# Weight-gradient chunks placed inside the last attention backward, and fourteen zero stores moved to the output phase

## The chip, the cores and the metric

The kernel runs on one core of one Trainium2 chip. A NeuronCore has five engines with an instruction stream each: TensorE (PE, with its weight loads shown apart as PEld), VectorE (DVE), ScalarE (ACT), GpSimd (POOL) and SyncE (SP), and 16 DMA engines that move data between the off-chip memory and the on-chip SBUF. Matrix products land in PSUM and are copied out of it by DVE or ACT. The metric is the device time of the whole program in microseconds (us); lower is better. Before the change it is 446.53 us, the median of 5 runs from 444.61 to 447.87 us.

## The reference

Two pre-norm layers, each an attention with a cached window and a dense block with a mish activation, are applied to a single token, twice, with the same weights; then everything is differentiated:

```python
def _fwd_reference(A_x, A_k_cache, A_v_cache, A_wq, A_wo, B_x, B_w1, B_b1, B_w2):
    def _A_ref(x, k_cache, v_cache, wq, wo):            # Hq 32, Hkv 4, Dh 128, Sk 32768
        W = min(4096, max(256, Sk // 4))                # only the last 4096 rows of the caches
        q = (lambda x, *d: x.transpose(*d))((x @ wq).reshape(B, Sq, Hq, Dh), 0, 2, 1, 3)
        k = jnp.repeat(k_cache[:, :, Sk - W:, :], rep, axis=1)
        v = jnp.repeat(v_cache[:, :, Sk - W:, :], rep, axis=1)
        scores = jnp.einsum("bhqd,bhkd->bhqk", q, k) * (Dh ** -0.5)
        p = _softmax(scores, axis=-1)
        o = jnp.einsum("bhqk,bhkd->bhqd", p, v)
        return (lambda x, *d: x.transpose(*d))(o, 0, 2, 1, 3).reshape(B, Sq, Hq * Dh) @ wo
    def _B_ref(x, w1, b1, w2):                          # D 1024, F 3584
        h = jnp.einsum("bsd,df->bsf", x, w1) + b1
        sp = jnp.log1p(jnp.exp(-jnp.abs(h))) + jnp.where(h > 0, h, jnp.zeros_like(h))
        return jnp.einsum("bsf,fd->bsd", h * jnp.tanh(sp), w2)
    x = A_x
    x = x + _A_ref(_layernorm(x), A_k_cache, A_v_cache, A_wq, A_wo)
    x = x + _B_ref(_layernorm(x), B_w1, B_b1, B_w2)
    ...
```

`reference` returns the output and the gradients of `A_x`, both caches, `wq`, `wo`, `w1`, `b1` and `w2`. With one token every weight gradient is a sum of two outer products (one for each use of the weight). The gradients of the caches are zero except in the last 4096 of 32768 rows, so the program must store 2 x 4 x 28672 rows of 128 bf16 zeros, 58.7 MB of the 170.13 MB that it moves.

## The kernel before, in words

The stages follow one another as a chain of small vectors: the forward layers A1, B2, A3, then `mlp_turn` (B4 forward and backward in one pass over `w1`), the backward of A3 (`attn_bwd` with `first=True`), a pass over `w2` (`W2Pass.rest`: the last forward product and the gradient of the hidden layer of B2), a pass over `w1` (`mlp_bwd_w1`), and the backward of A1 (`attn_bwd` with `first=False`), which ends in `g0`, the gradient of the input. In each stage the weights stream through a ring of 6 buffers of 512 KB (`st_tile`), loaded by SP's DMA queue. The kernel is written with the order of every engine's instructions by hand: what stands earlier in the code stands earlier in each engine's stream, and an engine takes its instructions in order.

**The zero stores.** The 112 zero stores of 512 KB each (128 rows of 4 KB) fill the DMA engines where a stage leaves them free. `bg_zeros(n, after)` (L180) issues n of them from POOL, after a tiny copy (`gate_t`) that waits for the tile `after`; `zeros(n)` (L167) issues them from SP; `zeros2(n)` (L171) takes two at once, 1 MB from a larger zero tile `area["zero"]`. The table `Z` (L1221) says how many go where: `B2a` and `B2` in the B2 stage, `A3`, `B4` by block of the B4 stage, `A3c` and `A3d` in the backward of A3, `B4w` by chunk of the `w2` pass, `W1m` by chunk of the `w1` pass, `A1c` and `A1d` in the backward of A1.

**The backward of A1** (L862 and on). It forms `do` from the incoming gradient `g_bf` and `wo` (functions `T` and `M`: transposes of the five `wo` chunks that are not kept, and products with them), multiplies it with V (`rows_mm`), forms `ds` from that (L990), multiplies `ds` with K (the PE line with `acc<-K`), copies the row, forms `dq` (L1011), multiplies it with `wq` (64 matmuls, `acc<-wq_b`), and ends in the layer norm's backward (`ln_bwd`). Beside that chain it prepares what the outer products need: `after_do` (L1195) cuts the SBUF space of `wo` into areas and clears two of them on POOL (L1200: the 2048 columns of the two spread tiles; L1202: the 4096 columns of `area["zero"]`); then five steps in the list `prep`, each of which is `spread_rows`: POOL copies a vector into a mostly zero spread tile, PE transposes it in 4 to 8 blocks (tile `rw`, L1046), and ACT copies the result to its place. `nextprep()` runs one such step after every `M` but the first, the last one after `rows_mm`. In gaps, `warm(n)` issues n matmuls of the identity with itself, whose result nobody reads.

**The output phase** begins after `g0`. PSUM is handed over to one pool of four pairs of banks (`pair`), and the list `jobs` runs: each job makes 4 matmuls (outer products with 2 rows of contraction), which fill two pairs, and two copies out of PSUM, one on DVE and one on ACT (`ev_out`), to half of a 1 MB staging slot, which SP stores after every second job; the jobs of `dkv` copy to their part of the tile `K`, which is stored in larger pieces. The jobs are, in this order: 14 for the gradient of `w2` (`dw_tall`, L1123) with 8 of the 16 for `w1` (`dw_wide`), the other 8 of `w1` woven with 8 of V's cache (`dkv`), 16 for `wo`, 16 for `wq` woven with 8 of K's cache. The gradient of K is stored only after its last job, 4 MB. Slots are taken in a ring: two in the space of `wo`, two of the weights' ring, two in V's space, and then the eight tiles of `wq_b`, put in after the last attention (L1315). The gradient of `wq` is staged in `wq_b` itself (`home`). The preparations for `wo`, V, K and `wq` (`late_prep`) stand between jobs.

Of the kernel before, what the change touches and what calls it, by code (L numbers as in the profile page):

```python
# [14 lines left out]
P = 128  # L15
HQ = 32
# [7 lines left out]
def kernel(  # L24
# [245 lines left out]

    def acc_tile(n):
        return pacc.tile([P, n], FP32, name="acc", tag="acc")

    def sm_tile(m, n):
        return pacc.tile([m, n], FP32, name="sm", tag="sm")

# [76 lines left out]
    def ln_bwd(dn_ps, n32, rstd, g_col, name, nxt):  # L353

        tt = work.tile([P, 2 * TD], FP32, name="tt")
        nc.vector.tensor_copy(tt[:, 0:TD], dn_ps)
        nc.vector.tensor_mul(tt[:, TD:], tt[:, 0:TD], n32[:])
        sps = sm_tile(P, 2 * TD)
        nc.tensor.matmul(sps[:], lhsT=onesD, rhs=tt[:], start=True, stop=True)
        if nxt == "A1":  # L360
            warm(5)
        if nxt == "B2":
            hook("ln")
        ab = work.tile([P, 2], FP32, name="ab")
        nc.vector.reduce_sum(ab[:], sps[:].rearrange("p (a b) -> p a b", a=2), axis=AX.X)
        t2 = work.tile([P, TD], FP32, name="t2")
        nc.vector.scalar_tensor_tensor(out=t2[:], in0=n32[:], scalar=ab[:, 1:2], in1=tt[:, 0:TD],
                                       op0=ALU.mult, op1=ALU.subtract, reverse1=True)
        gx = work.tile([P, TD], FP32, name="gx")
        nc.vector.tensor_scalar(out=gx[:], in0=t2[:], scalar1=ab[:, 0:1], scalar2=rstd[:, 0:1], op0=ALU.subtract, op1=ALU.mult)  # L370
        g_new = keep.tile([P, TD], FP32, name=f"g_{name}")
        nc.vector.tensor_add(g_new[:], g_col[:], gx[:])
        g_bf = pair_col("g" + nxt[0], nxt, TD)
        nc.vector.tensor_copy(g_bf, g_new[:])
        return g_new, g_bf
# [486 lines left out]
    def attn_bwd(g_col, g_bf, lname, sv, first, nxt):  # L862
# [30 lines left out]
        def M(i):  # L893
# [7 lines left out]
            if first and i in (1, 3, 5):  # L901
                fill(1, ["V", "K", "wq"], "a")
            if not first and i:
                nextprep()

# [10 lines left out]
        if not first:  # L916
# [6 lines left out]
                lambda: rows_put(area["R1"], 1, "dh", "pieces"),  # L923
            ])

        for i in range(2, len(late) + 1):
# [3 lines left out]
        if first:  # L930
            pre.extend(w2_load(c) for c in range(NB - 1))
            bg_zeros(Z["A3d"], g_bf)
            fill(100, ["V"])
        else:
            after_stream()
            zeros(Z["A1d"][0])
            zeros2(Z["A1d"][1])

# [30 lines left out]
        else:  # L969
            after_v()  # L970
            nc.sync.dma_start(area["p3"], out_5[0:P, :])
            nextprep(100)
            warm(3)
        scr = kp()
# [11 lines left out]
        dsT = kp().rearrange("p (j x) -> p j x", x=P)  # L986
        qrow = acc_tile(512)
        for hf in range(2):
# [3 lines left out]
        if first:  # L992
            fill(100, ["K"], "av")
        else:
            warm(4)
        for hf in range(2):
            half_T(ds, dsT, hf, "va"[hf])
        for j in range(TJ):
            for c in range(NC):
# [5 lines left out]
        else:  # L1005
            warm(3)
        qacc = sm_tile(P, HQ)
# [4 lines left out]
        if first:  # L1012
            fill(100, ["wq"], "av")
        nrow = acc_tile(512)
        for h in range(HQ):
            for half in range(2):
                row_mm(nrow, 2 * half + h % 2, dq_bf[:, h:h + 1],
                       wq_b[:, 4 * half:4 * half + 4, h // 16, (h % 16) * P:(h % 16 + 1) * P], h < 2, h >= HQ - 2)
        nps = sm_tile(P, TD)
        yr = rows_copy(nrow, "v")  # L1020
        if first:
# [14 lines left out]


    def spread_rows(n, put, dst, pairwise=False):

        sp = area["spread"][pools["sturn"] % 2]  # L1040
        pools["sturn"] += 1
        for l in range(2):
            put(sp.rearrange("p j (q x) -> p j q x", q=4), l)
        ps = psum1([P, 8, P], BF16, "rw")
        for j in range(n):
            nc.tensor.transpose(ps[:, j, :], sp[:, j, :], ident_bf[:])  # L1046
        o, i = dst, ps[:, 0:n, :].rearrange("p j x -> p (j x)")
        if pairwise:
            o, i = dst.rearrange("p (c x t) -> p c t x", x=P, t=2), ps[:, 0:n, :].rearrange("p (c t) x -> p c t x", t=2)
        evac(o, i, 0.69, 1.0, None if "pair" in pools else "a")  # L1050

# [143 lines left out]
    def after_do():  # L1195
# [3 lines left out]
        pools["sturn"] = 0  # L1199
        nc.gpsimd.memset(wo_flat[:, 0:2048], 0.0)  # L1200
        area["zero"], *more = cut_up(wo_flat, 8192, (4096,) * ((NR - 4) // 2))
        nc.gpsimd.memset(area["zero"], 0.0)  # L1202
        slots.extend(more)
# [12 lines left out]
    prep = []  # L1216
    def nextprep(n=1):
        for _ in range(min(n, len(prep))):
            prep.pop(0)()

    Z = dict(B2a=1, B2={0: 1, 4: 1, NW2 - 2: 4}, A3=14, B4=[3, 3, 2, 2, 2, 2, 5], A3c=6, A3d=28, B4w={1: 1, 4: 1, 13: 3}, W1=0, W1m=(8, 13), A1c=3, A1d=(7, 16))  # L1221

# [80 lines left out]

    g0, g0b = attn_bwd(g1, g1b, "A1", sA1, False, "X0")
    level()
    col_out(g0b, TD, out_1[0, 0, :])
    top(None)
    pacc.release()
    pt.release()
    pools["pair"] = ctx.enter_context(tc.tile_pool(name="pair", bufs=4, space=bass.MemoryType.PSUM))  # L1310

    def r3(nm):
        return area[nm].rearrange("p (g d) -> p g d", g=G)

    slots.extend(wq_b[:, t, :, :].rearrange("p h j -> p (h j)") for t in range(TD))  # L1315
    stage = {}

    def take(nm):
        stage[nm] = jobs[:]
        del jobs[:]  # L1320

    take("w")
    dkv(area["p3"], r3("do3"), sA1["p"], r3("do1"), out_3, True)
    take("v")
    dw_tall("wo", HQ, out_5.rearrange("(c p t) d -> c p t d", p=P, t=4))
    take("o")
    dkv(sA3["ds"], r3("q3"), sA1["ds"], r3("q1"), out_2, False)
    take("k")
    dw_wide(lambda: area["Rq"], 512, 2048, out_4, wq_t)
    take("q")  # L1330
    late_prep = [
        lambda: row_layout(sA3["dorep"], "do3"),
        lambda: row_layout(sA1["dorep"], "do1"),
        lambda: tall_left("wo", "o", 0),
        lambda: tall_left("wo", "o", 1),
        lambda: tall_right("wo", "gA"),
        lambda: row_layout(sA3["qrep"], "q3"),
        lambda: row_layout(sA1["qrep"], "q1"),
        lambda: rows_put(area["Rq"], 0, "nA", "rep"),
        lambda: rows_put(area["Rq"], 1, "dq", "heads"),  # L1340
        db1_out,
        x4_out,
    ]

    def weave(a, b, n):
        while a or b:
            jobs.extend(a[0:n])
            jobs.extend(b[0:1])
            del a[0:n], b[0:1]

    jobs.extend(stage["w"][:NW2 + 8])
    weave(stage["w"][NW2 + 8:], stage["v"], 1)
    jobs.extend(stage["o"])
    weave(stage["q"], stage["k"], 2)
    for at, f in zip((8, 11, 24, 27, 30, 40, 43, 46, 49, 51, 53), late_prep):
        jobs.insert(at, f)
    for at, n in ((24, 2), (27, 2), (33, 1)):
        jobs.insert(at, lambda n=n: zeros2(n))
    run(1000)
# [32 lines left out]
```

## Time and profile before

| What | Value |
|---|---|
| median of 5 runs | 446.53 us (444.61 to 447.87) |
| the profiled execution | 448.57 us |
| its span (first to last record) | 446.8 us |
| PE / DVE / ACT / POOL busy | 73% / 53% / 48% / 15% of the span |
| moved by DMA | 170.13 MB, mean 381 GB/s |
| zero stores from POOL / from SP in the backward of A1 / in the output phase | 84 / 24 / 4, in units of 512 KB |
| last copy out of PSUM ends | 432.34 us |
| last DMA ends | about 445.0 us |

The span is cut into stages by eye from the timeline: B2 from 68 to 112 us, A3 to 136, B4 to 196, the backward of A3 to 240, the `w2` pass to 264, the `w1` pass to 293, the backward of A1 to 333, and the output phase after it. In the rows of the profile, `out<-in` names the tile written and the tiles read; a bracket at the end of a timeline row says how long the engine was idle before it and what it waited for. PEclk is the clock that TensorE was granted, as a share of full speed. A DMA share near 1 means that all 16 DMA engines had packets in flight all the time.

### The profile page before, as it was taken

Reading aid. Unit: us, or ns where it says so; the run is one execution under the profiler, and the core shown is the slowest. Engines: PE = TensorE matmul, PEld = TensorE weight load, DVE = VectorE, ACT = ScalarE, POOL = GpSimd, SP = SyncE. Lnnn points to the kernel's source line nnn. Section 1 sums busy time; section 2 is a strip of 40 time slices with the busy share of each in tenths; the row PEclk is TensorE's granted clock in tenths of the full one; section 3 lists DMA queues with packets and bytes.
Section 4 is the critical chain, followed back from the end, with each engine's and each line's share of the span. In section 5 each row is a group of like instructions: output and inputs, shape, how many; then the busy total and the mean of one; then the engine's idle time right before and its main releaser. Section 6 shows DMA issues by size and latency. Waiting matters only on the chain. (4 is left out here: it accounts for less than half of the span.)

```text
span 446.8 us, 11638 instructions
## 1 busy us (share of the span) xinstructions
PE 324.2 (73%) x5020; PEld 222.3 (50%) x5020; DVE 235.2 (53%) x487; ACT 214.3 (48%) x253; POOL 66.4 (15%) x164
## 2 busy tenths in 40 slices
PE   1565755499898979898996577985967688675850
PEld 0343424389375979876875576864431132211110
DVE  3134101087252747675547473551439989897860
ACT  1122100065242857776855342523318877796860
POOL 2000000010520412242332010116010010000000
PEclk9989555565697988999998568867995555555555
DMA  7999999999999999999999999999978999999778
GB/s 319 422 420 414 407 399 375 385 347 387 373 406 355 370 352 351 376 409 407 415 407 382 416 350 366 298 400 419 425 316 343 419 418 413 396 415 395 307 305 352
DMA packets 44337, 170.13 MB, mean 381 GB/s; under 512 B 4449, under 2 KB 11645, under 8 KB 37501
## 3 DMA queue, kind: packets, MB, share of 16 engines
q1 hardware_dynamic: 31888, 124.79, 71.1%
q0 software_dynamic: 12352, 44.58, 25.5%
q8 instruction: 39, 0.64, 0.5%
q14 instruction: 14, 0.11, 0.1%
q10 hardware_dynamic: 44, 0.01, 0.0%
HBM read 70.27 MB, written 99.10 MB: 379 GB/s over the span
## 5 line engine op out<-in xcount | busy, mean ns | idle before, releaser
L278 PEld LDWEIGHTS <-ring 128*128 128x128 bf16 (+2 forms) x1828 | 60.0, 102 | 34.1 <-DMA ring<-in_B_w_dram 12.2
L195 ACT COPY ring<-tps 128x1024 bf16<-128x1024 bf16 (+1 forms) x40 | 37.6, 962 | 31.4 <-PE tps L242 31.2
L185 POOL DMA_DIRECT2D out_dram<-zt x84 | 44.5, 532 | 40.2 <-DMA out_dram<-zt 34.8
L242 PE MATMUL tps<-ident_bf,ring 128*128 128x128 bf16 x528 | 42.3, 240 | 4.9 <-DMA ring<-in_B_w_dram 4.8
L685 ACT COPY ring<-tps 128x1024 bf16<-128x1024 bf16 x28 | 28.3, 1012 | 31.6 <-PE tps L675 24.3
L698 DVE CUSTOM_DVE_ANT_0 ring<-ring,gbc 128x1024 bf16<-128x1024 bf16 x28 | 33.6, 1220 | 16.1 <-PE acc L278 15.1
L192 DVE CAST wq_b<-ops 128x1024 bf16<-128x1024 f32 (+1 forms) x36 | 39.2, 1126 | 4.4 <-DMA out_dram<-wq_b 2.7
L195 ACT CAST wq_b<-ops 128x1024 bf16<-128x1024 f32 (+1 forms) x40 | 38.3, 1014 | 5.6 <-PE ops L278 2.7
L242 PEld LDWEIGHTS <-ring 128*128 128x128 bf16 x528 | 35.6, 109 | 6.8 <-DMA ring<-in_B_w_dram 5.2
L278 PE MATMUL ops<-V 2*128 2x512 bf16 (+1 forms) x160 | 32.2, 603 | 5.7 <-DVE K L192 1.5
L192 DVE COPY ring<-tps 128x1024 bf16<-128x1024 bf16 (+1 forms) x30 | 19.6, 664 | 30.4 <-PE tps L242 30.3
L278 PEld LDWEIGHTS <-V 128*128 128x128 bf16 (+2 forms) x448 | 17.0, 102 | 33.0 <-issue 31.2
L278 PE MATMUL ops<-wo_b 2*128 2x512 bf16 x120 | 24.3, 557 | 8.2 <-ACT wq_b L195 3.0
L195 ACT COPY K<-tps 128x1024 bf16<-128x1024 bf16 x17 | 16.6, 1024 | 27.4 <-PE tps L242 27.4
L675 PE MATMUL tps<-ident_bf,ring 128*128 128x128 bf16 x224 | 25.6, 286 | 0.7 <-DMA ring<-in_B_w_dram 0.7
L278 PE MATMUL acc<-a_pair,ring 128*128 128x16 bf16 x448 | 15.9, 173 | 10.8 <-DMA ring<-in_B_w_dram 9.4
L192 DVE COPY K<-tps 128x1024 bf16<-128x1024 bf16 x15 | 10.2, 688 | 24.1 <-PE tps L242 24.1
L278 PEld LDWEIGHTS <-wo_b 2*128 2x128 bf16 (+1 forms) x232 | 9.1, 100 | 25.8 <-issue 23.6
L278 PE MATMUL q<-wq_b,nA_pair 128*32 128x512 bf16 x128 | 10.9, 465 | 14.9 <-DMA wq_b<-in_A_wq_dram 14.9
L195 ACT CAST K<-ops 128x1024 bf16<-128x1024 f32 x17 | 17.1, 1013 | 7.7 <-PE ops L278 7.5
L294 DVE COPY ring<-acc 128x512 f32<-128x512 f32 x6 | 4.1, 691 | 30.4 <-PE acc L278 30.4
L192 DVE CAST K<-ops 128x1024 bf16<-128x1024 f32 x15 | 18.3, 1221 | 3.3 <-PE ops L278 3.2
(319 smaller groups left out, 565.4 us busy)
## 6 DMA issues: line engine op xcount, KB each, us to landing
out_dram<-zt POOLq DMA_DIRECT2D x84, 512.0 KB, 10.1
ring<-in_B_w_dram SPq DMA_DIRECT2D x42, 512.0 KB, 7.7
ring<-in_B_w_dram SPq DMA_DIRECT2D x32, 448.0 KB, 6.4
out_dram<-wo_b SPq DMA_DIRECT2D x13, 1024.0 KB, 8.8
out_dram<-wq_b SPq DMA_DIRECT2D x12, 1024.0 KB, 5.1
ring<-in_A_wo_dram SPq DMA_DIRECT2D x20, 512.0 KB, 7.6
wq_b<-in_A_wq_dram SPq DMA_DIRECT2D x8, 1024.0 KB, 20.9
out_dram<-wq_b SPq DMA_DIRECT2D x7, 896.0 KB, 5.0
```

The lines of the kernel that those rows point to most:

```text
L185: nc.gpsimd.dma_start(zero_job(1), zt[:])
L192: nc.vector.tensor_copy(out_ap, in_ap)
L195: nc.scalar.copy(out_ap, in_ap)
L242: nc.tensor.transpose(ps[:, b, :], ap, ident_bf[:])
L278: nc.tensor.matmul(out_ap, lhsT=lhsT, rhs=rhs, start=start, stop=stop, skip_group_check=True, **kw)
L294: nc.vector.tensor_copy(yr, bank[:])
L675: nc.tensor.transpose(self.ps[c][:, b, :], w[:, 1, b * P:(b + 1) * P], ident_bf[:])
L685: nc.scalar.copy(self.w[c][:, 1, :], self.ps.pop(c)[:].rearrange("p b c -> p (b c)"))
L698: nc.vector.tensor_tensor_reduce(out=w[:, 0, :], in0=w[:, 0, :], in1=gbc[:], scale=1.0, scalar=0.0, op0=ALU.mult, op1=ALU.add, accum_out=s ...
```

## The change

Three things are done at once.

**Order inside the backward of A1.** `spread_rows` no longer finishes its step: POOL's copies are issued (`put_rows`), and PE's transposes with ACT's or DVE's copy are put in a list and issued later (`finish_rows`). The first two preparations start on POOL right after `after_do`, and all are finished after `rows_mm`. POOL clears the two spread tiles first (2 x 1024 columns); the 4096 columns of `area["zero"]` are cleared later, after the last preparation has been put. `nextprep` is gone.

**Jobs inside the backward of A1.** After `ds` a new function `tail()` (hook `tail`) releases the PSUM pools, opens `pair`, and builds the job list that used to be built after `g0`. One job of the gradient of `w2` runs at each of eight places from `ds` to after `g0`. Three `warm` calls (10 matmuls) are taken out. The tiles of `wq_b` join the slots after `wq` has been read for the last time.

**Zero stores.** Eight fewer are issued from POOL (three in B2, two in B4, two in the `w2` pass, one in the `w1` pass), six fewer from SP in the backward of A1 (18 of 512 KB in place of 8 of 512 KB and 8 of 1 MB). The output phase has 18 in place of 4: eight stores of 1 MB between jobs 16 and 46, and one of 1 MB behind the last store of K.

```diff
@@ T and M of attn_bwd
-            if not first and i:
-                nextprep()
@@ after the five preparations are listed
+            put_rows()
+            put_rows()
@@
             after_stream()
-            zeros(Z["A1d"][0])
-            zeros2(Z["A1d"][1])
+            zeros(Z["A1d"])
@@ after rows_mm with V
             nc.sync.dma_start(area["p3"], out_5[0:P, :])
-            nextprep(100)
-            warm(3)
+            finish_rows()
+            put_rows()
+            finish_rows()
+            put_rows()
@@ after ds
-            warm(4)
+            finish_rows()
+            put_rows()
+            nc.gpsimd.memset(area["zero"], 0.0)
+            hook("tail")
+            run(1)
         for hf in range(2):
             half_T(ds, dsT, hf, "va"[hf])
+        if not first:
+            finish_rows()
+            run(1)
+            qrow = acc_tile(512)
@@ after the copy of qrow
-            warm(3)
+            finish_rows()
+            run(1)
@@ before, in and after the 64 matmuls with wq
+        if not first:
+            run(1)
         nrow = acc_tile(512)
         for h in range(HQ):
+            if not first and h == HQ // 2:
+                run(1)
...
+        yr = rows_copy(nrow, "v")
+        if not first:
+            hook("wq")
+            run(1)
@@ ln_bwd, after its matmul
+        if nxt == "X0":
+            run(1)
@@ spread_rows
-        ps = psum1([P, 8, P], BF16, "rw")
-        for j in range(n):
-            nc.tensor.transpose(ps[:, j, :], sp[:, j, :], ident_bf[:])
...
+        def finish():
+            ps = psum1([P, 8, P], BF16, "rw")
+            for j in range(n):
+                nc.tensor.transpose(ps[:, j, :], sp[:, j, :], ident_bf[:])
...
+        ready.append(finish)
@@ after_do
-        nc.gpsimd.memset(wo_flat[:, 0:2048], 0.0)
+        for s in (s0, s1):
+            nc.gpsimd.memset(s, 0.0)
         area["zero"], *more = cut_up(wo_flat, 8192, (4096,) * ((NR - 4) // 2))
-        nc.gpsimd.memset(area["zero"], 0.0)
@@ the table
-    Z = dict(B2a=1, B2={0: 1, 4: 1, NW2 - 2: 4}, A3=14, B4=[3, 3, 2, 2, 2, 2, 5], A3c=6, A3d=28, B4w={1: 1, 4: 1, 13: 3}, W1=0, W1m=(8, 13), A1c=3, A1d=(7, 16))
+    Z = dict(B2a=0, B2={4: 1, NW2 - 2: 3}, A3=14, B4=[2, 2, 2, 2, 2, 2, 5], A3c=6, A3d=28, B4w={4: 1, 12: 2}, W1=0, W1m=(8,), A1c=3, A1d=18)
@@ the job list, now built in tail()
+        base = stage["w"][:NW2 + 8] + weave(stage["w"][NW2 + 8:], stage["v"], 1) + stage["o"] + weave(stage["q"], stage["k"], 2)
+        side = {
+            8: [lambda: row_layout(sA3["dorep"], "do3")],
+            10: [lambda: row_layout(sA1["dorep"], "do1")],
+            16: [lambda: zeros2(2)],
+            20: [lambda: tall_left("wo", "o", 0)],
+            21: [lambda: tall_left("wo", "o", 1)],
+            22: [finish_rows, lambda: zeros2(2)],
...
+            46: [lambda: zeros2(2)],
...
+        }
+    hooks.update(tail=tail, wq=lambda: slots.extend(wq_b[:, t, :, :].rearrange("p h j -> p (h j)") for t in range(TD)))
+    g0, g0b = attn_bwd(g1, g1b, "A1", sA1, False, "X0")
+    run(1)
+    col_out(g0b, TD, out_1[0, 0, :])
     run(1000)
     zeros2(1000)
```

## The prediction

> **What bounds the kernel now.** I read the slices of the span first. The DMA row stands at 9 almost everywhere, so the question is where it doesn't, and I then asked for the busy time of each engine by stretch from 292 us on (columns: stretch, its length, PE, PEld, DVE, ACT and POOL busy with counts, PE clock, DMA share, GB/s).
>
> ```profile
> PEclk9989555565697988999998568867995555555555
> DMA  7999999999999999999999999999978999999778
> ...
> 292.00:331.00 39.00, 30.93 (x422) 19.57 (x419) 14.39 (x37) 10.61 (x14) 10.31 (x28) 0.82 1.02 420
> 331.00:337.00 6.00, 3.05 (x21) 1.09 (x22) 4.42 (x10) 3.15 (x4) 1.71 (x9) 0.73 0.23 90
> 337.00:410.00 73.00, 52.86 (x321) 15.05 (x317) 64.68 (x78) 57.44 (x61) 2.92 (x12) 0.50 1.01 413
> 410.00:433.00 23.00, 18.20 (x104) 3.96 (x96) 20.32 (x18) 19.80 (x22) 0.00 (x0) 0.50 0.73 300
> 433.00:445.00 12.00, 0.00 (x0) 0.00 (x0) 0.00 (x0) 0.26 (x1) 0.00 (x0) 0.50 1.00 416
> ```
>
> The reader is to see two holes in a full DMA: 331 to 337, where the zero stores are used up and no gradient is ready, is idle for 0.77 x 6 = 4.6 us; 410 to 433, where DVE and ACT are the limit (20.3 and 19.8 of 23 us), for 0.27 x 23 = 6.2 us. After that 4 MB of K drain alone. Together 10.8 us of DMA time can be had; everything else from 292 us on is bound by bytes.
>
> Next the timeline of the backward of A1 and the chain of waits, for what makes these holes.
>
> ```profile
> 302.07 1.80 POOL L1200 MEMSET wo_b<- 128x2048 bf16 x1 [4.45 <-PE sm L278]
> 303.81 3.51 POOL L1202 MEMSET wo_b<- 128x4096 bf16 x1
> 307.99 1.03 PE L1046 MATMUL rw<-ident_bf,wo_b 128*128 128x128 bf16 x8 [4.91 <-POOL wo_b L1082]
> 321.09 1.91 PE L278 MATMUL acc<-K,ring 128*32 128x512 bf16 x32
> 325.20 3.64 PE L278 MATMUL acc<-wq_b,dq_pair 128*32 128x512 bf16 x64 [0.29 <-ACT dq_pair L1011]
> ...
> 399.08 5.61 DMA out_dram<-wq_b
> ```
>
> PE stands 4.91 us behind POOL's two clears, and the chain from `ds` to `g0` (319.3 to 332.6) leaves DVE and ACT nearly empty. At 399 the first chunk of `wq` waits 5.61 us for a slot that the gradient of `wo` still occupies.
>
> For the zeros that leave the earlier stages I looked at what PE waits for there.
>
> ```profile
> 73.39 0.54 PE L278 MATMUL acc<-nB_pair,ring 128*128 128x16 bf16 x14 [0.51 <-DMA ring<-in_B_w_dram]
> ...
> 246.74 0.58 PE L278 MATMUL acc<-a_pair,ring 128*128 128x16 bf16 x16 [2.20 <-DMA ring<-in_B_w_dram]
> ...
> 274.19 0.96 PE L242 MATMUL tps<-ident_bf,ring 128*128 128x128 bf16 x14 [2.32 <-DMA ring<-in_B_w_dram]
> ```
>
> Such waits are behind nearly every load from 72 to 88 us, sum to 8 us from 240 to 260, and come now and then to 291. From 136 to 196 PE waits 0.3 us in all for the ring: there the engines are the limit.
>
> **The change part by part.** A zero store of 0.524 MB costs 1.27 us of DMA at the 413 GB/s of 337 to 410.
>
> *Chain ahead of `ds`.* From the last product with `de` (303.1) to the last `M` (313.6) PE needs 10.5 us; of this 4.9 is the wait for POOL, and 18 of the 34 `rw` transposes and their copies on ACT stand between T and M. With both gone there remain two transposes of 8 (0.62), four products (0.35) and the copies between (ACT 1.02 and 1.01, DVE 0.69), some 3.3 us: `do` is 7.2 us earlier. On POOL the clears of the two spread tiles (1.80) and the first puts (1.18) end near 305, long before their transposes; the clear of 3.51 us now lies behind the last put, where POOL has nothing that anyone awaits before job 16. Cost nothing, hidden by the attention; if late, the first 1 MB zero store would wait and hold SP's later stores.
>
> *Chain from `do` to `g0`.* It gets the 34 transposes back (at 0.62 us for 8: 2.6 us), and loses 10 warm matmuls (0.81 + 1.04 + 0.82 = 2.7 us of PE). Seven jobs stand in it. One costs PE 0.61 us, DVE 1.22 and ACT 1.01. With only four pairs in PSUM each job also waits for the copies of the one before: the second half of a job after the 64 matmuls takes the pair that the copy of `nrow` frees, and a DVE copy of 1.22 us precedes the sums of the layer norm once. Laying these out one behind the other I get `ds` near 313, the matmuls with K at 316.4, with `wq` at 321.3 and from 323.7, `g0` near 331.8: 19 us became 25.5, so `g0` comes 0.8 us earlier, with three stores of 1 MB issued near 318, 322.5 and 328 and the fourth near 333.
>
> *The first hole.* Six fewer zeros on SP end the zeros at 331.2 - 6 x 1.27 = 323.6. With p3's load the three stores (2.5 us each) carry the DMA to 331.8; the fourth moves bytes at 334. So about 2.2 us stay idle, and with the first jobs, which make 1 MB in 2.5 us, just what the DMA takes, I count 2.5. Bounds: 1 (the stores overlap) and 8 (below).
>
> *The second hole.* Jobs 0 to 7 took 333.4 to 343.4 and are gone from the phase; the wait of 5.61 at 399 goes, since the slots of the last chunks of `wo` are no longer tiles of `wq_b` (the slots are now cut into before these tiles join). The last copy then ends near 432.3 - 10 - 4 = 418. DMA has the same bytes and 14 zeros more, so it is behind by some 8 MB when `wq` begins, more than the 2.6 MB (6.2 us) that it lacked. The hole is closed. After the last copy only K's 4 MB and 1 MB of zeros are new, 12.7 us: 431, well before the DMA's own end, so the 1 MB at the end costs only its bytes.
>
> *Bytes.* The six zeros of the A1 stage move within the full stretch: nothing. The eight from POOL add 8 x 1.27 = 10.2 us after 292.
>
> *What these eight give back ahead of it.* Each lies between 0 (stage bound by engines or ring slots) and 1.27 us (bound by DMA); below nothing is excluded, since a store taken away delays no load. By the waits above: `B2a` 1.0 (its neighbours all wait, but at 69 to 70 it fills a dip); the two at the ends of B2's `w2` pass 0.3 together (PE waits 1.3 us for the ring from 88 to 136); B4's two 0.5; `B4w` chunk 1, in the 8 us of waits, 1.2; the third of chunk 13, with the pair a chunk earlier, ahead of the waits of 2.32 and 0.96, 1.4; `W1m` 13, before waits of 0.43 and 1.09, 1.0. Sum 5.4, ends 0 and 10.2.
>
> *Sum.* -10.8 (holes) + 2.5 (new hole) + 10.2 - 5.4 = -3.5 us. The profiled execution took 448.57 with a span of 446.8, so 1.8 us lie around it and 445.1 is its sum; it stood 2.0 us above the median of the runs. From the median: 446.53 - 3.5 = 443.0.
>
> *A rule and a row on the PE clock.* In 336 to 447 the granted clock is 0.50 in every stretch though PE is 50 to 90% busy and nearly all of its gaps are under 1.3 us; that work is these very jobs. The Trainium skill ("TensorE: Matmul & The Clock Gate", Part 1) says that the clock is halved after an idle window of some 3.4 us and restored by as long of sustained work. By the rule the new chain, without a pause of that length, stays at full clock, even better than before (0.50 from 307 to 313, after the wait for POOL): 443.0. By the row, jobs in place of warm matmuls could take it to 0.50: both V and K products (1.91 each) and `wq`'s 3.64 double, 7.5 us, transposes some 1.5 more: the hole grows from 2.5 to 11.5, 452.0. I take the rule: jobs are 7 x 0.61 of 25 us here, the rest is dense.
>
> **The rivals.** (1) *Slower: the chain goes cold.* Place: PE clock from 308 to 332; price 9 us, 452.0. For it: the 0.50 of the output phase. Against: 25 us with few gaps, and full clock from 314 to 334 before. It decides when `g0` is later than forecast by more than 5.7 us (3.5 + 2.2). (2) *The early stores were hidden anyway:* the early stages give back only 1 us, 447.4, no change. For it: B4 and B2's `w2` pass hardly wait. Against: 2.20 and 2.32 us at the loads. (3) *Full relief:* DMA share is near 1 from 72 to 272, so backlog is handed from stage to stage and all 10.2 us come back: 438.2. Against: the dips at 266 and 278 us, where no store waits. That the jobs don't move is ruled out by the built order: eight groups of four `ops` matmuls stand before `g0`'s output.
>
> **How the numbers follow.** Forecast 0.58 (its own range 439.5 to 446), cold chain 0.13, no relief 0.12, full relief 0.17. The range 438 to 448 leaves out the cold chain and the edge of full relief. A measurement of this kernel tells some 0.5%, 2.2 us, from no change: faster is below 444.3. Of the forecast 0.50 lies there, with full relief 0.67; the same 0.08 + 0.10; slower 0.13 + 0.02.
>
> **What would show it.** Right: no idle of PE at the first `rw`; matmuls with K some 4 to 5 us earlier after `g_bf`; the DMA share near 1 in the last 40 us with no wait for a `wq_b` slot, last copy some 20 us before the last byte; the waits at loads from 72 to 88 and 240 to 291 shorter by 5 us, so that the backward of A1 begins near 290. Wrong: PEclk 0.5 in the 64 matmuls, a DMA hole over 6 us before the fourth store, or the A1 stage beginning at 294 or later.

## The result, and the profile after

The changed kernel takes 443.62 us (median of 44 runs, 438.68 to 448.49); the kernel before, measured beside it, takes 445.68 us (79 runs, 441.71 to 453.16). The ratio is 0.9948, with an interval from 0.9931 to 0.9966: 2.3 us faster, 1.5 to 3.1. Forecast were 3.5 us less, 443.0. The profiled execution took 443.72 us with a span of 441.9 us. Executions of both kernels fall into a faster and a slower state, and the ratio compares those of the faster one, so it is a little lower than the quotient of the two medians; the profiled execution of before, 448.57 us, is one of the slower ones, so lengths of stages are read with those of other kernels beside them.

The slices of the span after the change, PE clock and DMA share:

```profile
PEclk9998565575697998996998588988775555555555
DMA  7999999999999999999999999999969999999997
```

Before, the DMA row had 7 and 8 at the first hole and 7, 7, 8 at the end. Now one 6 is left at the first hole, and a 7 in the last slice, which is the end itself. Busy time by stretch in the changed kernel (columns as in the prediction):

```profile
292.00:321.00 29.00, 25.16 (x319) 12.61 (x311) 15.84 (x30) 12.65 (x17) 8.51 (x25) 0.82 1.03 411
321.00:323.00 2.00, 1.34 (x10) 1.27 (x10) 1.52 (x4) 0.69 (x1) 0.00 (x0) 1.00 0.34 143
323.00:326.00 3.00, 1.17 (x14) 0.33 (x13) 2.37 (x7) 1.93 (x2) 0.00 (x0) 0.92 0.85 350
326.00:332.00 6.00, 5.46 (x29) 1.24 (x25) 6.00 (x13) 4.88 (x5) 1.70 (x9) 0.50 0.70 284
332.00:400.00 68.00, 53.15 (x318) 15.12 (x317) 61.61 (x70) 55.90 (x60) 2.74 (x12) 0.50 1.01 413
400.00:430.00 30.00, 9.69 (x58) 2.10 (x53) 12.13 (x11) 11.25 (x12) 0.00 (x0) 0.50 1.01 419
```

The first hole is 0.66 x 2 + 0.15 x 3 + 0.30 x 6 = 3.6 us, and the second is gone: the DMA share is 1.01 from 332 to 430. DVE and ACT are busy for only 12 and 11 of the 30 us from 400 on, because their work is done early; before, they were the limit in that stretch. The chain of waits says the same: its last long pieces are stores, and the chunk behind them is the end of the copies.

```profile
376.48 14.37 DMA out_dram<-wq_b
...
390.92 18.60 DMA out_dram<-wq_b
...
409.57 0.81 DVE wq_b L192
```

The last copy out of PSUM ends at 413 us in place of 432.34; the DMA engines then drain what they are behind. No DVE or ACT copy waits for a `wq_b` slot any more. The backward of A1, in the timeline of the changed kernel:

```profile
293.78 1.84 POOL L1233 MEMSET wo_b<- 128x1024 bf16 x2 [3.77 <-PE sm L282]
...
301.49 0.96 PE L1076 MATMUL rw<-ident_bf,wo_b 128*128 128x128 bf16 x14
...
304.21 3.51 POOL L1004 MEMSET wo_b<- 128x4096 bf16 x1
304.50 0.40 PE L282 MATMUL ops<-wo_b 2*128 2x512 bf16 x4 [1.43 <-DVE V L997]
...
307.53 3.60 PE L282 MATMUL acc<-K,ring 128*32 128x512 bf16 x32
...
314.65 3.01 PE L282 MATMUL acc<-wq_b,dq_pair 128*32 128x512 bf16 x32
...
318.13 2.17 PE L282 MATMUL acc<-wq_b,dq_pair 128*32 128x512 bf16 x32
```

PE no longer stands at the first `rw` transposes, and the clear of 3.51 us lies where nobody waits for it. But the products with K take 3.60 us (1.91 before) and those with `wq` 3.01 + 2.17 = 5.18 (3.64 before): the clock was at 0.50 for part of the chain.

### The profile page after: what moved, and what is told of

Read it like the earlier page. It is cut to its first block, busy times and chain, and to the rows that moved or that the text cites. A ratio compares the mean times of both kernels' runs of the same rounds, so it can differ in the third digit from the quotient of the medians.

```text
span 441.9 us, 11636 instructions
## 1 busy us (share of the span) xinstructions
PE 319.0 (72%) x5010; PEld 217.3 (49%) x5010; DVE 235.4 (53%) x489; ACT 212.3 (48%) x251; POOL 61.1 (14%) x153
## 5 line engine op out<-in xcount | busy, mean ns | idle before, releaser
L282 PEld LDWEIGHTS <-ring 128*128 128x128 bf16 (+2 forms) x1828 | 58.7, 101 | 34.3 <-DMA ring<-in_B_w_dram 12.2
L185 POOL DMA_DIRECT2D out_dram<-zt x76 | 40.2, 532 | 38.8 <-DMA out_dram<-zt 34.5
L242 PE MATMUL tps<-ident_bf,ring 128*128 128x128 bf16 x528 | 39.2, 230 | 5.4 <-DMA ring<-in_B_w_dram 3.6
L195 ACT CAST wq_b<-ops 128x1024 bf16<-128x1024 f32 (+1 forms) x36 | 34.9, 1012 | 3.1 <-PE ops L282 3.0
L242 PEld LDWEIGHTS <-ring 128*128 128x128 bf16 x528 | 32.7, 103 | 7.2 <-DMA ring<-in_B_w_dram 4.0
L192 DVE CAST wq_b<-ops 128x1024 bf16<-128x1024 f32 (+1 forms) x28 | 30.6, 1120 | 0.8 <-PE ops L282 0.8
L681 PE MATMUL tps<-ident_bf,ring 128*128 128x128 bf16 x224 | 23.9, 273 | 0.7 <-DMA ring<-in_B_w_dram 0.7
L192 DVE COPY K<-tps 128x1024 bf16<-128x1024 bf16 x15 | 10.2, 688 | 24.4 <-PE tps L242 24.4
L192 DVE CAST K<-ops 128x1024 bf16<-128x1024 f32 x16 | 19.5, 1220 | 3.8 <-PE ops L282 3.6
L242 PE MATMUL tps<-ident_bf,K 128*128 128x128 bf16 x256 | 19.7, 236 | 0.5 <-ACT K L195 0.3
L242 PEld LDWEIGHTS <-K 128*128 128x128 bf16 x256 | 16.6, 106 | 6.0 <-issue 5.4
```

The lines of the kernel that those rows point to most:

```text
L185: nc.gpsimd.dma_start(zero_job(1), zt[:])
L192: nc.vector.tensor_copy(out_ap, in_ap)
L195: nc.scalar.copy(out_ap, in_ap)
L242: nc.tensor.transpose(ps[:, b, :], ap, ident_bf[:])
L282: nc.tensor.matmul(out_ap, lhsT=lhsT, rhs=rhs, start=start, stop=stop, skip_group_check=True, **kw)
L681: nc.tensor.transpose(self.ps[c][:, b, :], w[:, 1, b * P:(b + 1) * P], ident_bf[:])
```

## The experiments

All ratios are to the kernel before, measured on the same chip in the same session. `gA_pair` is the tile written as the backward of A1 starts, `gX_pair` the one written with `g0`.

**The eight zeros back in the early stages.** Jobs and order stay as changed.

```diff
-    Z = dict(B2a=0, B2={4: 1, NW2 - 2: 3}, A3=14, B4=[2, 2, 2, 2, 2, 2, 5], ..., B4w={4: 1, 12: 2}, W1=0, W1m=(8,), A1c=3, A1d=18)
+    Z = dict(B2a=1, B2={0: 1, 4: 1, NW2 - 2: 4}, A3=14, B4=[3, 3, 2, 2, 2, 2, 5], ..., B4w={1: 1, 4: 1, 13: 3}, W1=0, W1m=(8, 13), A1c=3, A1d=18)
```

> The changed kernel with the eight zero stores back in B2, B4, the w2 and the w1 pass; the output phase has 10 in place of 18. Theory (the new order closes the two DMA holes, 10.8 us becoming 3.8, and the moved stores only cost what the early stages do not give back): the holes stay closed, since the copies out of PSUM have 26 us of lead at the end of the changed kernel and lose 8 x 1.27 = 10 of it; so 7 us below the kernel before, a ratio of 0.984, faster than the changed kernel by 2 to 5 us. Rival (the gain comes from the early stages, which run without these stores): the gain is gone, ratio 1.00.

Measured: 437.11 us, ratio 0.9773 (0.9732 to 0.9814), faster than both kernels. Against the changed kernel's 0.9948 this is 7.8 us less, where the forecast's terms give 10.2 - 5.4 = 4.8. Read alone it would mean that the early stages give back only 2.4 us; it was measured again below.

**The order inside the backward of A1 alone.** The kernel before with the preparations put and finished as in the change and the late clear of `area["zero"]`, but with the `warm` calls kept, no job before `g0`, and the early zeros where they were. It also takes over how the changed kernel issues the 24 zeros of the backward of A1 (512 KB each) and where it puts the later preparations between the jobs.

```diff
-            if not first and i:
-                nextprep()
...
+            put_rows()
+            put_rows()
...
-            nextprep(100)
+            finish_rows()
+            put_rows()
+            finish_rows()
+            put_rows()
             warm(3)
```

> The kernel before with the new order of the preparations alone (put early, finished after rows_mm, the large clear behind the last put; warm matmuls kept, jobs after g0, zeros distributed as before with 24 of 512 KB in the backward of A1). Theory: g0 comes 5 to 6 us earlier after g_bf, the hole of 4.6 us before the first gradient store nearly closes, the hole of 6.2 us in the last stage stays: 4.6 us less, ratio 0.990. Rival (the wait for POOL was covered, or what it frees is lost again at the slot of wq): ratio 1.00.

Measured: 445.66 us, ratio 0.9976 (0.9950 to 1.0001). `gX_pair` comes 28.7 us after `gA_pair` (37.3 before; 35.9 and 36.6 in the next kernel and in that of the slots alone, which keep the old order), so the order alone takes 7.2 to 8.6 us out of the chain, and the first hole closes. Yet the gain is 1.1 us, not clear of none. Waits and stretches of this kernel:

```profile
ACT wq_b L195 <- DMA out_dram<-wq_b: 7.9, 1, 7.9
```

```profile
312.00:345.00 33.00, 23.39 (x203) 8.34 (x193) 23.58 (x35) 19.73 (x23) 3.37 (x10) 0.68 1.02 419
...
400.00:433.00 33.00, 21.31 (x120) 4.91 (x119) 25.33 (x22) 24.62 (x26) 0.00 (x0) 0.50 0.76 315
```

The 7.9 us are the wait for the slot of the first chunk of `wq` (2.7 in the same list of before; the 5.61 in its chain of waits is the whole store, of which the copies waited for the end). The work comes earlier, the stores do not, so the slot is waited for longer, and 0.24 x 33 = 7.9 us of DMA time are lost after 400.

**The zeros alone.** The kernel before with the eight zeros moved to the output phase.

```diff
-    Z = dict(B2a=1, B2={0: 1, 4: 1, NW2 - 2: 4}, ..., B4=[3, 3, 2, ...], ..., B4w={1: 1, 4: 1, 13: 3}, ..., W1m=(8, 13), ...)
+    Z = dict(B2a=0, B2={4: 1, NW2 - 2: 3}, ..., B4=[2, 2, 2, ...], ..., B4w={4: 1, 12: 2}, ..., W1m=(8,), ...)
-    for at, n in ((24, 2), (27, 2), (33, 1)):
+    for at, n in ((24, 2), (27, 2), (33, 2), (42, 2), (50, 2), (58, 2)):
```

> The kernel before with the eight zero stores moved alone: B2, B4, w2 and w1 as in the changed kernel, four more stores of 1 MB between the jobs of the output phase; order and jobs as before. Theory: the early stages give back 5 to 8 us, the output phase takes 10.2 more of DMA time and some 3.5 of it falls into the hole of the last stage: +1 us, between -1 and +3, ratio 1.002. Rival (the stores are the gain): 3 us or more less, ratio 0.993.

Measured: 454.38 us, ratio 1.0136 (1.0089 to 1.0183). The wait for the slot in this kernel:

```profile
ACT wq_b L195 <- DMA out_dram<-wq_b: 12.5, 1, 12.5
```

The new zeros at 50 and 58 stand among the jobs of `wo`, the others ahead of them, all before the stores that free the slots, and the wait is 12.5 us. Order alone and zeros alone come to -0.0024 + 0.0136 = +0.0112, 5.0 us slower; all three parts together are 2.3 us faster. Some 7 us must come from what neither of these two has.

**No job in the chain.** The changed kernel without its eight `run(1)` and with the three `warm` calls back. It was meant to keep the slots in the changed order, by a rotation of the list.

```diff
-            run(1)
+            warm(4)
...
+    def wq_slots():
+        slots[:] = slots[3:] + slots[:3]
+        slots.extend(wq_b[:, t, :, :].rearrange("p h j -> p (h j)") for t in range(TD))
```

> The changed kernel without jobs inside the backward of A1: all 78 run after g0, and the 10 warm matmuls stand where they stood before; order of the preparations, zeros and order of the slots as in the changed kernel. Theory of bytes (DMA alone sets the end, the copies have more lead than they need): g0 comes some 6 us earlier after g_bf, the first store about where the fourth was, the hole stays at 2 to 4 us, and the lead of the copies shrinks from 26 to about 18 us: within 1.5 us of the changed kernel, ratio to before 0.995. Rival (the jobs in the chain are the gain): the copies end 8 us later and the time goes back to that of before or above, ratio 1.00 to 1.01.

Measured: 455.89 us, ratio 1.0169 (1.0125 to 1.0214). The rotation did not do what it should: the last chunks of `wo` were again in tiles 0 to 2 of `wq_b`, where the gradient of `wq` begins:

```profile
ACT wq_b L195 <- DMA out_dram<-wq_b: 18.6, 1, 18.6
```

So two things differ from the changed kernel, the jobs and the slots, and this run can't tell them apart. The next three do.

**The slots alone.** The kernel before; only the moment changes at which the `wq_b` tiles join the slots.

```diff
-    slots.extend(wq_b[:, t, :, :].rearrange("p h j -> p (h j)") for t in range(TD))
...
+    stage["w"].insert(6, lambda: slots.extend(wq_b[:, t, :, :].rearrange("p h j -> p (h j)") for t in range(TD)))
```

> The kernel before, in which only the moment changes at which the wq_b tiles join the staging slots: after the third chunk of the w2 stage, as the order of the slots then has the last three chunks of wo in the ring, V and wo instead of wq_b tiles 0 to 2. No instruction is removed and no zero store is moved. Theory (the wait for the wq_b slot behind the last chunks of wo opens the tail hole): the wait of 5.6 us goes and with it the hole of 6.2 us at 410 to 433; the first hole of 4.6 us stays. Time lower by 5 to 6 us, ratio about 0.987 (0.983 to 0.992). Rival (the slots' order is of no account; the hole is closed by the jobs that went into the chain): ratio 1.00 (0.997 to 1.003) and the hole stays.

Measured: 442.57 us, ratio 0.9930 (0.9898 to 0.9963). The direction is the theory's, the size about half of it and outside its range. A stretch of this kernel:

```profile
400.00:428.00 28.00, 20.55 (x113) 4.55 (x109) 23.14 (x21) 22.85 (x24) 0.00 (x0) 0.50 0.88 365
```

No copy waits for a `wq_b` slot, but the tail hole does not close: 0.12 x 28 = 3.4 us are left of 6.2. Without jobs done earlier DVE and ACT are still at the limit there (23.1 and 22.9 of 28 us). This one line moved is worth 3.1 us, about as much as the whole change (2.3).

**No job in the chain, slots as in the changed kernel.**

```diff
         side = {
+            6: [lambda: wq_slots()],
             8: [lambda: row_layout(sA3["dorep"], "do3")],
...
-        slots[:] = slots[3:] + slots[:3]
...
-    hooks.update(tail=tail, wq=wq_slots)
+    hooks.update(tail=tail)
```

> The kernel of the run without jobs in the chain, with the warm matmuls back, but the wq_b tiles join the slots so that the last chunks of wo use the same tiles as in the changed kernel. The eight zeros wait in the output phase. Theory (the slots' order made that run slow): the wait for the wq_b slot of 17 us goes, the tail hole closes, and what is left against the changed kernel is the first hole, 8 us in place of 3.8: ratio about 1.004 (0.998 to 1.008). Rival (the jobs in the chain are the gain themselves, through the ten us of output work that are done early): stays at about 1.017 (1.012 to 1.021).

Measured: 445.55 us, ratio 0.9982 (0.9941 to 1.0023), against 1.0169 with the other slots, in another session: some 8 us from the order of the slots alone, about twice what sessions differ by (0.009, below). Stretches:

```profile
312.00:325.00 13.00, 9.01 (x85) 3.46 (x78) 7.99 (x15) 5.67 (x7) 1.71 (x9) 0.74 0.56 224
...
400.00:430.00 30.00, 11.03 (x62) 2.41 (x59) 13.52 (x12) 12.63 (x14) 0.00 (x0) 0.50 1.01 421
```

The tail is full without any job in the chain. What the jobs do is in the first row: without them the hole after the last small zero is 0.44 x 13 = 5.7 us, with them 3.6 in the changed kernel. The chain is shorter without them, 31.4 us from `gA_pair` to `gX_pair` in place of 37.9, so part of what the jobs fill they also lengthen. How much of that is the clock is shown below.

**The old slots in the changed kernel.**

```diff
-    hooks.update(tail=tail, wq=lambda: slots.extend(wq_b[:, t, :, :].rearrange("p h j -> p (h j)") for t in range(TD)))
+    def wq_slots():
+        slots[3:3] = [wq_b[:, t, :, :].rearrange("p h j -> p (h j)") for t in range(TD)]
+
+    hooks.update(tail=tail, wq=wq_slots)
```

> The changed kernel, jobs and zeros as they are, with the wq_b tiles put into the slots at such a place that the last three chunks of wo are again in wq_b tiles 0 to 2. Theory: the wait for the wq_b slot is back, with a tail hole of 5 to 7 us: ratio about 1.008 (1.003 to 1.014). Rival (with the jobs done early the wait has no effect, since the copies run far ahead of the stores): stays at 0.995 (0.992 to 0.998).

Measured: 447.82 us, ratio 1.0034 (0.9996 to 1.0072); the changed kernel has 0.9948, and the kernel without jobs and with the changed slots 0.9982 in the same session. The wait is back with the jobs in place:

```profile
ACT wq_b L195 <- DMA out_dram<-wq_b: 22.1, 1, 22.1
```

```profile
400.00:436.00 36.00, 21.13 (x120) 5.03 (x119) 25.66 (x22) 24.82 (x26) 0.00 (x0) 0.50 0.76 314
```

The tail hole is back too, 0.24 x 36 = 8.6 us. The difference to the changed kernel's 0.9948, 3.8 us, lies between two sessions and is by itself just under what they differ by; it is the wait and the hole in the trace that tell. Copies that run ahead do not make up for it: the earlier they come, or the later the stores, the longer the slot is waited for (2.7, 7.9, 12.5, 18.6 and 22.1 us in before and these four kernels), and the lead is lost.

**How the eight zeros share the cost, and the first measurement again.** Five back in B2 and B4 (the first diff's `B2a`, `B2` and `B4`), or three back in the `w2` and `w1` passes (its `B4w` and `W1m`), or all eight, the kernel of the first experiment, on one chip.

> The changed kernel with the three zero stores of B2 and the two of B4 back in these stages; the three of the w2 and w1 passes stay in the output phase. By the terms of the forecast these five give back only 1.8 of their 6.35 us when they are taken away, so that their return is worth 4.5 us: ratio 0.985. If all eight late zeros cost 7 to 8 us and not 4.8 because B2 and B4 give back nothing at all: 6.35 us, ratio 0.981. If the excess lies in the w2 and w1 passes, 0.985 holds here and it shows in the other kernel.

Measured: 438.67 us, ratio 0.9858 (0.9813 to 0.9903).

> The changed kernel with the three zero stores of the w2 and w1 passes back in these stages; the five of B2 and B4 stay in the output phase. By the terms of the forecast these three give back 3.6 of their 3.8 us, so that their return is worth nothing: ratio 0.994. If they give back little, as the excess in the w2 and w1 passes would have it: 2 to 3.5 us better, ratio 0.987 to 0.990.

Measured: 442.65 us, ratio 0.9921 (0.9883 to 0.9959).

> The changed kernel with all eight zero stores back in the early stages, once more, on the chip and beside the runs of the two kernels with a part of them. If the first measurement holds: ratio 0.977 (0.973 to 0.982). If it was too good by the spread of its few runs: 0.984, what the forecast's give-back of 5.4 us would make of it.

Measured: 439.19 us, ratio 0.9861 (0.9818 to 0.9904).

The repeat is 0.009 above the first measurement, and the two intervals don't meet. So an interval from one session says too little about another: between sessions I read no difference under some 0.009. The mean of both is 0.982, 5.8 us under the changed kernel's 0.9948; the forecast's terms say 4.8. All four kernels with the eight zeros early, in three sessions, lie between 0.977 and 0.986. Among these three kernels, measured side by side, leaving the three of `w2` and `w1` late costs nothing (0.9858 beside 0.9861; forecast 0.2 us), and leaving the five of B2 and B4 late costs 0.006, 2.7 us with some 2.6 to either side (forecast 4.5). The terms stand within what can be told. The waits of PE's products for loads in the `w2` pass are shorter in the changed kernel; before, and then changed, from 240 to 286 us:

```profile
PE acc L278 <- DMA ring<-in_B_w_dram: 8.1, 7, 2.2
```

```profile
PE acc L282 <- DMA ring<-in_B_w_dram: 5.2, 4, 3.1
```

In the `w1` pass, where PE waits ahead of transposes, nothing is seen: 3.3 us before, 3.6 changed. `gA_pair` is written between 291.1 and 294.1 us in five kernels with the zeros early (mean 292.3) and between 286.8 and 291.0 in four with them late (mean 288.5), 3.8 us apart (before, the first measurement and the old slots, read in longer executions, are left out: 295.3, 296.0 and 290.7). How the return divides between the stages is not settled: with five late it is written at 287.6, with three late at 291.7, the reverse of the forecast's split, but single executions of one class are 3 to 4 us apart.

**Six more small zeros in the backward of A1.** The kernel of the first experiment with `A1d=24`.

```diff
-    Z = dict(..., A1c=3, A1d=18)
+    Z = dict(..., A1c=3, A1d=24)
```

> The changed kernel with the eight zeros back in the B2, B4, w2 and w1 stages, and six more of the small zeros in the backward of A1, 24 in all, so that four are left to the output phase. Theory: the DMA hole of 4.4 us in the chain of that run is filled with stores that the output phase no longer has to make, so the time falls by a further 3 to 4.5 us: ratio about 0.968 (0.963 to 0.974). Rival (the hole lies between the last small zero and the first chunk whatever their number, since the queue that issues them is behind): ratio as without them, 0.977 (0.973 to 0.981).

Measured: 437.95 us, ratio 0.9813 (0.9762 to 0.9864), no less than the mean of 0.982 without them. The hole is filled, and in the profiled executions the last DMA ends 140.9 us after `gA_pair`, against 144.5 without them; the timed runs don't show these 3.6 us. The hole is gone in this execution, as the theory has it, but one kernel without the six has none either (below); a gain in time is not shown.

**The pause before the first job.** The same kernel without the six, and six warm matmuls in the 1.4 us that PE stands before `ds` is there.

```diff
             nc.gpsimd.memset(area["zero"], 0.0)
+            warm(6)
             hook("tail")
```

> The same kernel with all eight zeros early, and six warm matmuls put before the first job, where TensorE now stands 1.4 us until ds is there. Theory (this pause takes the clock down to 0.50 for the products with K): the 32 matmuls with K take 1.9 us in place of 3.6, the eight transposes 0.6 in place of 1.0, g0 comes some 2 us earlier and the first DMA hole is shorter by as much: ratio lower by 0.003 to 0.005 than without them. Rival (the clock falls because the jobs have two rows of contraction, whatever the pauses): K stays at 3.6 us and the ratio as without them.

Measured: 438.23 us, ratio 0.9829 (0.9778 to 0.9881), beside 0.9861 (0.9818 to 0.9904) without them on the same chip: not told apart. The profile tells more. Stretches and timeline without the warm matmuls:

```profile
325.00:330.00 5.00, 3.31 (x40) 1.78 (x33) 3.17 (x6) 1.85 (x2) 0.00 (x0) 1.00 0.54 224
330.00:336.00 6.00, 4.36 (x25) 1.13 (x24) 5.86 (x18) 4.33 (x6) 1.71 (x9) 0.61 0.65 262
```

```profile
313.24 3.61 PE L282 MATMUL acc<-K,ring 128*32 128x512 bf16 x32
```

And with them:

```profile
304.00:312.00 8.00, 7.28 (x108) 4.07 (x106) 6.33 (x10) 4.93 (x7) 5.56 (x15) 1.00 1.03 416
312.00:322.00 10.00, 8.92 (x96) 4.29 (x92) 5.55 (x6) 5.00 (x6) 0.00 (x0) 0.83 1.03 420
```

```profile
305.29 1.46 PE L201 MATMUL wps<-ident_bf 128*128 128x512 bf16 x6
...
309.28 1.91 PE L282 MATMUL acc<-K,ring 128*32 128x512 bf16 x32
...
314.36 3.52 PE L282 MATMUL acc<-wq_b,dq_pair 128*32 128x512 bf16 x32
```

With the pause filled the products with K take 1.91 us and not 3.61, and `gX_pair` comes 16.1 us after the first of them in place of 18.2. But the clock falls all the same, a little later: the first half of the products with `wq` takes 3.52 us in place of 1.91. Nor do the pause and the thin job behind it (outer products with two rows) bring the fall by themselves. The kernel with the old slots has the same PE instructions in this chain as the changed one, pause included, and no fall:

```profile
306.46 0.40 PE L282 MATMUL ops<-wo_b 2*128 2x512 bf16 x4 [1.43 <-DVE V L997]
...
308.87 1.91 PE L282 MATMUL acc<-K,ring 128*32 128x512 bf16 x32
...
313.92 1.91 PE L282 MATMUL acc<-wq_b,dq_pair 128*32 128x512 bf16 x32
```

And the kernel without jobs and with the changed slots has a fall with no job in the chain and no pause over 0.6 us in the four us ahead of it, while the same pause further on, with warm matmuls behind it, brings none:

```profile
297.72 3.56 PE L282 MATMUL d<-V,do_pad 128*32 128x512 bf16 x32
...
304.78 1.04 PE L201 MATMUL wps<-ident_bf 128*128 128x512 bf16 x4 [1.40 <-DVE V L996]
...
306.64 1.91 PE L282 MATMUL acc<-K,ring 128*32 128x512 bf16 x32
```

So neither the theory nor the rival is shown. The kernels side by side, one execution each, in us (products with V and K, the two halves of those with `wq`, the chain from `gA_pair` to `gX_pair`, the first DMA hole):

| Kernel | V | K | `wq` | chain | hole |
|---|---|---|---|---|---|
| old slots | 1.91 | 1.91 | 1.91, 1.91 | 33.0 | none |
| eight zeros early, six warm | 1.91 | 1.91 | 3.52, 1.91 | 34.3 | none |
| five zeros early | 1.91 | 2.94 | 3.20, 1.91 | 35.7 | 1.3 |
| three zeros early | 1.91 | 3.55 | 3.56, 1.91 | 37.2 | 2.2 |
| changed | 1.91 | 3.60 | 3.01, 2.17 | 37.9 | 3.6 |
| eight zeros early, again | 3.42 | 3.61 | 3.00, 2.19 | 39.7 | 4.4 |

But for the six warm matmuls, PE has the same instructions in this chain in all six. What differs is where the clock falls, and with it the chain's length and the first hole. Reading the clock in steps of half a microsecond, I find it go down or up at 288.0, 291.4, 305.1, 311.9, 315.3, 318.7 and 325.6 us in the changed kernel: all distances are multiples of some 3.41 us. The same spacing holds within each other trace that shows more than one change, but the moments lie elsewhere against the chain. So the clock seems to be set once per 3.41 us, at moments that the program doesn't choose, and a fall costs such a span or two of them at half speed. That reading fits every trace here; no run was made to test it.

## Why the prediction was right, and where a step was off

**The sum.** It was -10.8 (holes) + 2.5 (new hole) + 10.2 - 5.4 = -3.5 us. With the measured first hole of 3.6 us in it, it is -2.4; measured were -2.3 (-3.1 to -1.5). The mis-sized term is the new first hole, 1.1 us too small. That the rest then fits to a tenth is luck: the hole is that of one execution, and with 5.8 for the zeros' net cost in place of 4.8 the sum is -1.4.

**The first hole, and the clock behind it.** The chain was forecast 0.8 us shorter; `gX_pair` comes 37.9 us after `gA_pair` in place of 37.3, 1.4 us later than the step said, which is about the hole's excess. Two errors stand against each other in it, and that they nearly cancel is luck too. The order was summed at -7.2 + 2.6 (the transposes back) = -4.6 us, and gave -8.6 (-7.2 and -7.9 when taken from the zeros alone and the slots alone, whose chains in the old order take 35.9 and 36.6 us). Jobs in place of warm matmuls were then +3.8, and are 37.9 - 28.7 = +9.2. Most of these 5.4 us too many are the clock: where it stays at 1.00, in the kernel with the old slots, the chain takes 33.0 us and the jobs cost 33.0 - 28.7 = +4.3, near the forecast. The forecast weighed the rule of the Trainium skill ("TensorE: Matmul & The Clock Gate", Part 1: half clock after an idle window of some 3.4 us), by which the chain stays warm, against the row of the output phase, by which it all runs at 0.50 and costs 9 us, and took the rule. Neither held: from 301 to 319 PE's longest pause is the 1.43 us above, and the clock still fell; its falls cost the chain 37.9 - 33.0 = 4.9 us, between 0 and 9. The measurement decides over the rule: PE was busy for 1.99 of the 3.42 us before the fall at 305.1, and for 2.52 of the 3.42 us before the fall at V in the kernel without jobs and with the changed slots. How much work is enough is not settled: with the old slots 1.99 of 3.41 us were followed by full clock.

**The second hole.** That it closes was right. Two causes were given: jobs 0 to 7 leave the phase, and the slots of the last chunks of `wo` are no longer tiles of `wq_b`. The 5.61 us given as the wait are the length of the store; the copies waited 2.7. The runs weigh the causes. With the slots changed and no job in the chain the tail is full when the late zeros are there too, 1.01 from 400 to 430; with all jobs in the chain and the old slots 8.6 us of it are idle, and the kernel is at 1.0034, no faster than before. The slots decide. They are a side effect: the `wq_b` tiles are put in later, when jobs have already taken turns from the list, and so stand at another place in the ring. The slots alone gain 3.1 us and leave 3.4 of the hole's 6.2; the early jobs, or late zeros as DMA work for that time, are needed for the rest. The prediction did not say that, without the slots, both other parts gain nothing or lose: order alone gains 1.1 us, not clear of none, and zeros alone cost 6.1.

**The zeros.** Their 10.2 us of bytes in the output phase against 5.4 us given back: net +4.8 forecast, 5.8 by the mean of two measurements. Of the rivals, full relief (net 0) falls; no relief (net 9.2) is within the spread of the first measurement (7.8, with 1.8 to either side) and far from the second (3.9), so it is less likely but not ruled out. So the zeros' move is the part of the change that loses, and the kernel without it is at 0.9773 and 0.9861 in two measurements, 8 us below before by their mean.

**What was named as a sign.** No idle of PE at the first `rw`: so. K 4 to 5 us earlier after `g_bf`: 19.9 us after `gA_pair` in place of 25.8, 5.9 earlier. Last copy some 20 us before the last byte: at 413, with the last DMA near 439, 26 us. Waits at loads 5 us shorter: 8.9 to 8.0 us from 72 to 88 and 12.9 to 8.8 from 240 to 291 for PE's products and transposes, 5.0 in all; but the kernel with the slots alone, whose zeros are those of before, has 7.7 and 11.0, so one execution does not tell. Backward of A1 near 290: 287.7. No hole over 6 us: 3.6. One sign of being wrong came in part: the clock was 0.50 for much of the 64 products with `wq`.

## What to carry to other kernels

Where a ring of staging slots shares its space with the destination of a later stage, look at which slots the last chunks before that stage land in: one line that put tiles into the ring later was worth 3.1 us in one session and some 8 between two, more than moving work, and with the wrong slots work brought forward was lost as a longer wait. A store moved out of a stage is worth only what the stage's waits for loads give back, so a move of background stores is summed by stage, and measured in pairs with and without it, beside the change of order it comes with. The same chain of instructions took 33.0 to 39.7 us with the clock, so read the duration of the dense products in several executions before a few microseconds of one profile are put down to a change.

## What the runs showed that was not expected

- The clock of TensorE fell to 0.50 inside a chain without a pause over 1.43 us, for 3.4 or 6.8 us at a time and at other places in each execution, and stayed at 1.00 in one execution of the same PE instructions. Filling the pause did not remove the fall. In the output phase the clock stays at 0.50 with PE 78% busy (53.15 of 68 us). What exactly it counts is not settled by these runs.
- Ratios of one and the same kernel, each with 6 to 8 runs of its own, were 0.9773 and 0.9861 on two chips, with intervals of 0.004 to either side. A few per mille between sessions are no difference here.
